# Two decoder layers with cached attention: scores from key tiles by TensorE column groups in place of VectorE products, one pair at a time

## The chip, the core and the metric

The kernel runs on one core of a Trainium2 chip. The metric is the device time of one execution in microseconds (us). The kernel before was run three times: 1359.86, 1361.52 and 1363.43 us, median 1361.52 us.

## What is computed

Two rows of activations (batch B = 2, one new token each, D = 448) go through the same two blocks twice: attention over a cache of 4096 keys and values in each of 16 heads (head size 256), and a gated feed-forward block (F = 1792). All is float32.

```
def _A_ref(x, k_cache, v_cache, wq, wo):          # attention, H = 16, Dh = 256
    q = (x @ wq).reshape(B, Sq, H, Dh).transpose(0, 2, 1, 3)
    scores = einsum("bhqd,bhkd->bhqk", q, k_cache) * (Dh ** -0.5)
    o = einsum("bhqk,bhkd->bhqd", softmax(scores), v_cache)
    return o.transpose(0, 2, 1, 3).reshape(B, Sq, H * Dh) @ wo
def _B_ref(x, W_gate, W_up, W_down):              # feed-forward
    gate, up = x @ W_gate, x @ W_up
    return ((gate * (gate > 0)) * up) @ W_down
x = x + _A_ref(layernorm(x), ...); x = x + _B_ref(layernorm(x), ...)
x = x + _A_ref(layernorm(x), ...); x = x + _B_ref(layernorm(x), ...)
```

The second layer uses the same caches and weights as the first, and all of them together are far larger than on-chip memory, so nearly everything is read from HBM twice.

## The kernel before

**Pairs and pieces.** The work of one layer's attention is 32 pairs (head, batch row). Keys and values of a pair are 4 MB each. Each is cut into four pieces of 128 partitions x 2048 floats (1 MB; 8 KB in each partition): partition p holds 32 consecutive keys, a piece is 8 of them, each of 256 numbers.

**Places.** A tile `arena` has 27 places of one piece: 6 blocks of 4 and 3 singles (`BLOCKS`, `SINGLES`). A load takes a place, or a whole free block when four pieces are loaded by one DMA (`grouped`); it is put on SyncE's queue (SP) by `pump`, which runs each time that a piece is given back (`release`). So the loads stand in one fixed list, `pending`, and each is issued when its turn has come and its places are free. The list is: head weights, keys of pair 0, keys of pair 1, values of pair 0, keys of pair 2, values of pair 1 and so on, then the eleven weight pieces of the feed-forward block (seven `in`, four `out`), and the same for layer two, whose pairs run in reverse order. The first 13 and the last 12 pieces of a layer's caches go singly where the rules `SMALL` and `ENDS` say so.

**Kept pieces.** Because layer two starts with the pairs on which layer one ended, some pieces stay in the arena and are not loaded again: `KEPT = 20` pieces of keys and values and one more piece of values, and the weights of one head. While they lie there, 5 of the 27 places are left for loads.

**Scores.** `score(u, c)` works on piece c of pair u. VectorE multiplies the piece by the query, which stands on all 128 partitions (L360, one instruction of 2048 numbers per partition), then VectorE sums five of the eight keys (L365) and ScalarE three (L362). For kept pieces, whose contents must survive, VectorE does eight fused multiply-and-sum instructions instead (L354). The query is brought to all partitions by a TensorE product with 33 columns, a ScalarE copy and two GpSimd broadcasts (`query`), or by TensorE with the row repeated 128 times (`query_of`).

**Softmax, values, output.** `softmax_max` and `softmax_exp` find the maximum (VectorE, GpSimd), the exponentials (ScalarE, L378 and L381) and their sum (GpSimd). `weigh` multiplies with the values on TensorE, four products of 2 x 512 per piece in four column groups of the array (L401: `po[32*t : 32*t+2]`). `out_copy`, `out_add`, `out_turn`, `out_keep`, `project` bring a pair's result through `wo` into `acc` (L414, L417, L425, L434, L444). `absorb` adds the result to the activations, `squares` and `deviation` do the layer norm, `ffn` the feed-forward block (L498 for gate and up, L525 and L527 turn the hidden row, L568 and L573 for down).

**Order.** The order is written by hand. Step u of the loop at L463 scores pair u, weighs pair u-1 and turns and projects pair u-2, interleaved, so a layer's end is two steps behind its last scores. `busy` issues TensorE products into `po_all` whose results nobody reads (L222): 8 squares of 128 x 128 after each piece of the last two weighed pairs of a layer, and a few before the feed-forward block.

Of the kernel before, what the change touches and what calls it, by code (L numbers as in the profile page):

```python
# [8 lines left out]
F32 = mybir.dt.float32  # L9
# [14 lines left out]
KEPT = 20  # L24
# [4 lines left out]
BY_ACT = 3  # L29
HEAD = FULL * DH + P + 2 * D  # L30
# [35 lines left out]
def two_layers(  # L66
# [19 lines left out]
    ps_f = ctx.enter_context(tc.tile_pool(name="ps_f", bufs=2, space=PSUM))  # L86
# [10 lines left out]
    def source(key, n):  # L97
        kind, name, c = key
        if kind in "kv":
            h, b = name  # L100
            rows = (k_cache if kind == "k" else v_cache)[b, h]
            return rows.rearrange("(p t) d -> p (t d)", t=NT)[:, c * UNIT : (c + n) * UNIT]
# [65 lines left out]
    keep.add(("v", second[2], NC - 1))  # L168
# [9 lines left out]
    junk = consts.tile([P, DH], F32, name="junk")  # L178
# [22 lines left out]
    xs = consts.tile([P, DC, 33], F32, name="xs")  # L201
    nc.vector.memset(xs, 0.0)
    xr = xs[:, :, :32].rearrange("p c (b r) -> p c b r", b=B)
# [7 lines left out]


# [3 lines left out]

    def busy(n, half):


        for k in range(0, n, 4):  # L220
            m = min(4, n - k)
            nc.tensor.matmul(  # L222
                po_all[:B, half, : m * P], ident[:, :B],
                ident[:, None, :].to_broadcast([P, m, P]), start=True, stop=True,
            )
# [10 lines left out]
    def absorb(rows, n, rhs, nrhs):  # L236


        sums = work.tile([P, 1], F32, name="sums")
        nc.scalar.activation(row[:n, :D], rows, AF.Copy, accum_out=sums[:n])  # L240
        minus = ps_s.tile([P, B], F32, name="small")
        nc.tensor.matmul(minus, sums[:n].to_broadcast([n, P]), nrhs[:n], start=True, stop=True)
        pt = ps_s.tile([P, DC, B], F32, name="small")
        turned(pt, row[:n], rhs[:n], start=True, stop=True)
        less = work.tile([P, B], F32, name="less")
        nc.vector.tensor_copy(less, minus)
        for part in (less[:, None, :].to_broadcast([P, DC, B]), pt):
# [3 lines left out]
        nc.vector.tensor_copy(xs[:, :, 32:], xs[:, :, 31:32])  # L251
# [20 lines left out]
    def attention(order, after, begun):  # L272
# [8 lines left out]
        def query_of(u, pq):  # L281
            h, b = order[u]
            w = get("h", h, 0)
            for c in range(FULL):
                nc.tensor.matmul(  # L285
                    pq[:, b, :],
                    xT[:, c, b : b + 1].to_broadcast([P, P]),
                    w[:, c * DH : (c + 1) * DH],
                    start=(c == 0),
                    stop=False,  # L290
                )
            for j in range(2):
                nc.tensor.matmul(
                    pq[:, b, j * P : (j + 1) * P],
                    xT[:, FULL + j, b : b + 1].to_broadcast([P, P]),
                    w[:, FULL * DH : FULL * DH + P],
                    start=False,
                    stop=(j == 1),
                )
            q_of[u] = pq[:, b, :]  # L300

        def query(u):
            h = order[u][0]
            w = get("h", h, 0)
            pq = ps_q.tile([P, B, DH], F32, name="pq")
            if ("h", h, 0) in after:
                for v in (u, u + 1):
                    query_of(v, pq)
                return


            q = pq[:33, 0, :]
            for c in range(FULL):
                nc.tensor.matmul(  # L314
                    q, xs[:, c, :], w[:, c * DH : (c + 1) * DH], start=(c == 0), stop=False
                )
            for j in range(2):
                nc.tensor.matmul(  # L318
                    q[:, j * P : (j + 1) * P],
                    xs[:, FULL + j, :],  # L320
                    w[:, FULL * DH : FULL * DH + P],
                    start=False,
                    stop=(j == 1),
                )
            found = w[:33, DH : 2 * DH]
            nc.scalar.activation(found, q, AF.Copy)  # L326
            for v in (u, u + 1):
                b = order[v][1]
                q_of[v] = w[:, 2 * b * DH : (2 * b + 1) * DH]
                nc.gpsimd.partition_broadcast(q_of[v], found[32 * b : 32 * b + 1], channels=P)  # L330

        def first_query():


            total = squares()
            pq = ps_q.tile([P, B, DH], F32, name="pq")
            w = get("h", order[0][0], 0)
            for u, at in ((0, HEAD), (1, 0)):
                query_of(u, pq)
                nc.scalar.activation(w[:, at : at + DH], q_of[u], AF.Copy)  # L340
                q_of[u] = w[:, at : at + DH]
                if u == 0:
                    deviation(total)
            nc.scalar.activation(nsr[:, :1], eps_t, AF.Exp)

        def score(u, c):
            kt = get("k", order[u], c).rearrange("p (t n) -> p t n", t=CT)
            if c == 0:
                s_of[u] = work.tile([P, NT], F32, name="scores")
            kept = ("k", order[u], c) in after  # L350
            found = s_of[u][:, c * CT : (c + 1) * CT]
            if kept or ahead and u < ahead:
                for t in range(CT):
                    nc.vector.scalar_tensor_tensor(  # L354
                        junk if kept else kt[:, t, :], kt[:, t, :], 1.0, q_of[u],
                        op0=ALU.mult, op1=ALU.mult, accum_out=found[:, t : t + 1],
                    )
            else:

                nc.vector.tensor_mul(kt, kt, q_of[u][:, None, :].to_broadcast([P, CT, DH]))  # L360
                for t in range(BY_ACT):
                    nc.scalar.activation(  # L362
                        kt[:, t, :], kt[:, t, :], AF.Copy, accum_out=found[:, t : t + 1]
                    )
                nc.vector.reduce_sum(found[:, BY_ACT:], kt[:, BY_ACT:, :], axis=AX.X)  # L365
            if not kept:
                release("k", order[u], c)
# [25 lines left out]
        def weigh(u, c):  # L393
# [16 lines left out]
            if u >= n_u - 2:  # L410
                busy(8, (u + 1) % 2)
# [24 lines left out]
        def project(u):  # L436
# [11 lines left out]
            if u == n_u - 1:  # L448
                busy(5, 0)
# [8 lines left out]
        begun()  # L458

        ahead = 2 if ("k", order[0], 0) in keep else 0  # L460
        if ahead:
            query(ahead)
        for u in range(n_u + 2):  # L463
            if_pair(score, u, 0)
            if u == 0:
                inverse()
                nc.vector.tensor_scalar_mul(sr, rstd, SCALE)
                nc.vector.tensor_scalar_mul(nsr, rstd, -SCALE)
            if_pair(out_add, u - 2)
            if_pair(out_turn, u - 2)  # L470
            if_pair(score, u, 1)
            if_pair(score, u, 2)
            if_pair(out_keep, u - 2)
            if_pair(project, u - 2)
            if u % 2 and ahead < u + 1 < n_u:
                query(u + 1)
            if_pair(softmax_sum, u - 1)
            if_pair(score, u, 3)
            if_pair(softmax_max, u)
            if_pair(softmax_exp, u)  # L480
            for c in range(NC):
                if_pair(weigh, u - 1, c)
            if_pair(out_copy, u - 1)

    def ffn(last):
# [3 lines left out]
        busy(2, 0)  # L489
        total = squares()  # L490

        def proj(parts):

            p = ps_f.tile([P, D], F32, name="pf")
            for n, (part, c, done) in enumerate(parts):
                w = get("in", "", part)
                for j in range(4):
                    nc.tensor.matmul(  # L498
                        p[32 * j : 32 * j + 32, :],
                        xs[:, c, :32],  # L500
# [10 lines left out]
        pg = proj([(0, 0, True), (1, 1, True), (2, 2, True), (3, 3, False)])  # L511
# [8 lines left out]
        pu = proj([(3, 4, True), (4, 0, True), (5, 1, True), (6, 2, True)])  # L520
        nc.vector.tensor_mul(hid, pu, hid)

        ph = ps_f.tile([P, 4, P], F32, name="pf")
# [19 lines left out]
        else:  # L543
# [3 lines left out]
            near = work.tile([P, FULL, 4, B], F32, name="near")  # L547
# [4 lines left out]
            near_tails = work.tile([P, 2, B], F32, name="near_tails")  # L552
# [6 lines left out]
        pd = ps_f.tile([P, D], F32, name="pf")  # L559
# [39 lines left out]
def _arrays(np, A_x, A_k_cache, A_v_cache, A_wq, A_wo, B_W_gate, B_W_up, B_W_down, **_):  # L599
# [11 lines left out]
    chunks += [np.concatenate([down[j, rows:], down[j + 1, rows:]]) for j in (0, 2)]  # L611
    found = {
        "x": A_x,
        "k_cache": A_k_cache,
# [30 lines left out]
```

## Time and profile before

| what | value |
|---|---|
| runs of the kernel before | 1359.86, 1361.52, 1363.43 us |
| the profiled execution: span from first to last instruction | 1357.3 us |
| VectorE busy (DVE) | 1012.7 us, 75% |
| TensorE busy (PE) | 583.2 us, 43% |
| ScalarE busy (ACT) | 407.8 us, 30% |
| mean clock granted to TensorE | 0.681 of full speed |
| bytes of the load queue | 562.58 MB |

The page of the profiled execution gives its span, not its time by the host's measure, so 2.6 to 6.1 us of the three times shown lie around the span. Of the trace, the most telling view here is the table of stretches: for chosen stretches it gives the busy time of each engine, the granted clock of TensorE (PEclk), the share of the time that the DMA engines were busy and the rate at which they moved bytes. A timeline row gives start, duration, engine, line, operation, what it writes and reads, and in brackets how long its engine had idled and what ended that. In the trace a float32 product is two MATMUL and two weight-load records.

### The profile page before, as it was taken

The page shows a single profiled execution, that of the slowest core. Times are in us where ns is not written, and L with a number is a line of the kernel's source. Part 1 is how long each engine was busy: PE and PEld are TensorE (multiplying, and loading weights), DVE is VectorE, ACT ScalarE, POOL GpSimd, SP SyncE. Part 2 cuts the span into 40 slices and gives each one's busy share as a digit, 9 for nine tenths or more (in the row PEclk, how much of TensorE's full clock was granted, in tenths as well). Part 3 has the DMA queues.
Part 4 walks back from the last instruction along what each step waited for, and adds up shares of the span by engine and source line. Part 5 has one row for each costly group of instructions (what it writes and reads, how often), then busy time and mean ns, then how long its engine had stood idle before and what let it go on. Part 6 is the DMA issues. An engine that isn't in the chain of part 4 may idle for free.

```text
span 1357.3 us, 10287 instructions
## 1 busy us (share of the span) xinstructions
PE 583.2 (43%) x3122; PEld 189.5 (14%) x3122; DVE 1012.7 (75%) x1183; ACT 407.8 (30%) x1733; POOL 106.8 (8%) x192
## 2 busy tenths in 40 slices
PE   2433424434334444245773444434434434334368
PEld 2111101111101111012130111111101111111112
DVE  4987787777877877877339999987877877877861
ACT  2333333333333333320011333333333333333321
POOL 0210000000000000000001111110000000000010
PEclk9767566667667666567796666666566667666679
DMA  9999999999999999999879999999999999999994
GB/s 400 434 431 430 432 430 432 430 429 431 431 430 432 430 430 429 431 428 424 344 307 361 402 431 432 433 429 429 431 427 434 429 430 433 429 428 436 422 421 167
DMA packets 29294, 563.22 MB, mean 415 GB/s; under 512 B 3252, under 2 KB 3384, under 8 KB 10168
## 3 DMA queue, kind: packets, MB, share of 16 engines
q1 hardware_dynamic: 29236, 562.58, 97.3%
q8 instruction: 24, 0.39, 0.1%
q14 instruction: 30, 0.25, 0.0%
q10 hardware_dynamic: 4, 0.00, 0.0%
HBM read 562.56 MB, written 0.00 MB: 414 GB/s over the span
## 4 chain that ended last, share of the span: by engine, by line
DMA 53%; DVE 32%; PE 11%; ACT 2%; issue 2%; DVEq 0%; POOL 0%; SPq 0%; POOLq 0%; ACTq 0%
DMA arena<-in_k_cache_dram 52%; DVE arena L360 16%; DVE scores L365 11%; PE pq L314 2%; PE po L222 2%; PE acc L444 2%; DVE junk L354 2%; DVE arena L354 1%; PE po L401 1%; ACT arena L362 1%; DVE row L417 1%; PE pf L498 1%; DMA arena<-in_w_out_dram 1%; PE pq L285 1%; PE pq L318 1%
## 5 line engine op out<-in xcount | busy, mean ns | idle before, releaser
L360 DVE TENSOR_TENSOR arena<-arena 128x2048 f32<-128x2048 f32 x236 | 539.4, 2285 | 152.1 <-DMA arena<-in_k_cache_dram 147.3
L362 ACT ACTIVATE arena<-arena 128x256 f32<-128x256 f32 x708 | 286.0, 405 | 538.5 <-DVE arena L360 538.5
L401 PE MATMUL po<-arena,probs 128*2 128x512 f32 x2048 | 315.1, 738 | 122.3 <-DMA arena<-in_v_cache_dram 112.6
L365 DVE TENSOR_REDUCE scores<-arena 128x5 f32<-128x1280 f32 x236 | 350.7, 1486 | 8.2
L425 PE MATMUL small<-ones,row 128*128 128x1 f32 x256 | 62.2, 347 | 416.3 <-DVE row L417 416.3
L444 PE MATMUL acc<-arena,oT 128*2 128x448 f32 x128 | 51.6, 905 | 195.0 <-DVE oT L434 195.0
L362 ACT ACTIVATION_READ_ACCUMULATOR arena<-arena 128x1 f32 x708 | 132.5, 187 | 0.0
L425 PEld LDWEIGHTS small<-ones,row 128*128 128x128 f32 x256 | 56.7, 309 | 477.1 <-DVE row L417 477.1
L401 PEld LDWEIGHTS po<-arena,probs 128*2 128x2 f32 x2048 | 54.6, 96 | 318.1 <-issue 307.6
L373 POOL PARTITION_ALL_REDUCE top<-mx x64 | 51.5, 805 | 595.0 <-DVE mx L371 595.0
L314 PE MATMUL pq<-arena,xs 128*33 128x256 f32 x174 | 75.1, 599 | 13.8 <-DMA arena<-in_w_head_dram 12.6
L330 POOL PARTITION_BROADCAST arena<-arena x58 | 30.0, 587 | 536.1 <-ACT arena L326 509.6
L371 DVE TENSOR_REDUCE mx<-scores 128x1 f32<-128x32 f32 x64 | 11.9, 186 | 69.6 <-ACT arena L362 66.1
L378 ACT ACTIVATE nm<-top,nsr 128x1 f32<-128x1 f32 x64 | 18.8, 294 | 146.4 <-POOL top L373 146.4
L417 DVE SCALAR_TENSOR_TENSOR row<-po,ri,row 128x256 f32<-128x256 f32 x64 | 30.5, 477 | 39.5 <-ACT row L414 39.4
L326 ACT ACTIVATE arena<-pq 33x256 f32<-33x256 f32 x29 | 10.9, 377 | 140.6 <-PE pq L318 140.6
L414 ACT ACTIVATE row<-po,ri 128x256 f32<-128x256 f32 x64 | 29.6, 462 | 52.1 <-PE po L222 38.0
L314 PEld LDWEIGHTS pq<-arena,xs 128*33 128x33 f32 x174 | 25.5, 163 | 82.9 <-issue 80.1
L222 PE MATMUL po<-ident 128*2 128x512 f32 (+2 forms) x76 | 36.9, 609 | 0.0
L354 DVE SCALAR_TENSOR_TENSOR junk<-arena,pq 128x256 f32<-128x256 f32 x64 | 26.9, 420 | 8.0 <-DMA arena<-in_k_cache_dram 6.0
L444 PEld LDWEIGHTS acc<-arena,oT 128*2 128x2 f32 x128 | 3.0, 82 | 197.7 <-DVE oT L434 197.7
L385 POOL PARTITION_ALL_REDUCE total<-rs x64 | 24.6, 385 | 61.7 <-ACT probs L381 61.7
(105 smaller groups left out, 284.0 us busy)
## 6 DMA issues: line engine op xcount, KB each, us to landing
arena<-in_k_cache_dram SPq DMA_DIRECT2D x57, 4096.0 KB, 44.7
arena<-in_v_cache_dram SPq DMA_DIRECT2D x57, 4096.0 KB, 53.0
arena<-in_w_head_dram SPq DMA_DIRECT2D x31, 896.0 KB, 39.4
arena<-in_v_cache_dram SPq DMA_DIRECT2D x19, 1024.0 KB, 19.9
arena<-in_k_cache_dram SPq DMA_DIRECT2D x16, 1024.0 KB, 9.1
arena<-in_w_in_dram SPq DMA_DIRECT2D x14, 896.0 KB, 18.6
arena<-in_w_out_dram SPq DMA_DIRECT2D x4, 896.0 KB, 13.0
arena<-in_w_out_dram SPq DMA_DIRECT2D x3, 672.0 KB, 7.8
```

Source lines behind the costliest of these rows:

```text
L222: nc.tensor.matmul(po_all[:B, half, : m * P], ident[:, :B], ident[:, None, :].to_broadcast([P, m, P]), start=True, stop=True,)
L314: nc.tensor.matmul(q, xs[:, c, :], w[:, c * DH : (c + 1) * DH], start=(c == 0), stop=False)
L330: nc.gpsimd.partition_broadcast(q_of[v], found[32 * b : 32 * b + 1], channels=P)
L354: nc.vector.scalar_tensor_tensor(junk if kept else kt[:, t, :], kt[:, t, :], 1.0, q_of[u], op0=ALU.mult, op1=ALU.mult, accum_out=found[:, ...
L360: nc.vector.tensor_mul(kt, kt, q_of[u][:, None, :].to_broadcast([P, CT, DH]))
L362: nc.scalar.activation(kt[:, t, :], kt[:, t, :], AF.Copy, accum_out=found[:, t : t + 1])
L365: nc.vector.reduce_sum(found[:, BY_ACT:], kt[:, BY_ACT:, :], axis=AX.X)
L373: nc.gpsimd.partition_all_reduce(mx_of[u], mx, P, RED.max)
L401: nc.tensor.matmul(po_of[u][32 * t : 32 * t + 2, :], p_of[u][:, n : n + 2], vt[:, 2 * t * DH : (2 * t + 2) * DH], start=(c == 0), stop=(c ...
L417: nc.vector.scalar_tensor_tensor(row[:, :DH], po_of.pop(u)[:, DH:], r_of[u][:, 1:2], row[:, :DH], op0=ALU.mult, op1=ALU.add,)
L425: nc.tensor.matmul(pT_of[u][:, c : c + 1], row[:, c * P : (c + 1) * P], ones, start=True, stop=True,)
L444: nc.tensor.matmul(acc[at : at + B], oT_of[h][:, c, :], wo[:, c * D : (c + 1) * D], start=(n < 3), stop=(n >= n_u - 3),)
```

## The change

Keys are laid out on the host so that a piece holds, on partition p, number p (and number 128 + p) of each of 1024 keys. The query is made as a column: `query` multiplies the head's weights (as the stationary operand) with the activations and copies a 128 x 4 result from PSUM. `score` is then 8 TensorE products per piece: the query column is stationary (one column), 256 keys move, two halves of the head are added up, and four groups of keys go to four column groups of the array, rows 0, 32, 64 and 96 of the PSUM tile `raw`. The piece is given back as soon as these are done. VectorE copies 128 x 256 of `raw` (of which four rows matter) to `found_s`, and `score_turn` turns that with two TensorE products of 128 x 4 per piece into the layout that the softmax had before. The multiplication and sums on VectorE and ScalarE are gone, as are the GpSimd broadcasts.

The loop does a pair from scores to weighing in one step: scores, softmax, then output steps of the pair before, the next query, then weighing, and in the list of loads the values of a pair follow its keys. `busy` and its products are gone. `KEPT` is 22 (the extra piece of values is dropped), so 22 pieces and one head stay and 4 places are left. The feed-forward block uses `raw` in place of two PSUM tiles of its own.

```diff
-KEPT = 20
+KEPT = 22
+G, E = 4, 2
+QN = E * P
...
         for u, unit in enumerate(order):
             found.append(("k", unit, 0))
-            if u > 0:
-                found.append(("v", order[u - 1], 0))
             if u % 2 and u + 1 < len(order):
                 found.append(("h", order[u + 1][0], 0))
-        return found + [("v", order[-1], 0)]
+            found.append(("v", unit, 0))
+        return found
...
-    keep.add(("v", second[2], NC - 1))
...
+            pq = ps_q.tile([P, 2, B], F32, name="pq")
+            for j in range(2):
+                for c in range(FULL):
+                    at = c * DH + j * P
+                    nc.tensor.matmul(
+                        pq[:, j, :], w[:, at : at + P], xT[:, c, :], start=(c == 0), stop=False
+                    )
...
+            nc.vector.tensor_copy(q, pq)
...
         def score(u, c):
...
+            kt = get("k", order[u], c).rearrange("p (j g n) -> p j g n", j=2, g=G)
+            half, at = c % 2, c // 2 * QN
+            for j in range(2):
+                for g in range(G):
+                    nc.tensor.matmul(
+                        raw[32 * g : 32 * g + 1, half, at : at + QN],
+                        q_of[u][:, j, :], kt[:, j, g, :], start=(j == 0), stop=(j == 1),
+                    )
+            if ("k", order[u], c) not in after:
+                release("k", order[u], c)
+            nc.vector.tensor_copy(found_s[:, half, :], raw[:, half, at : at + QN])
+
+        def score_turn(u, c):
...
+            for e in range(E):
+                n = c * CT + e * G
+                nc.tensor.matmul(
+                    s_of[u][:, n : n + G], found_s[:, c % 2, e * P : (e + 1) * P], pick,
+                    start=True, stop=True,
+                )
...
-            if u >= n_u - 2:
-                busy(8, (u + 1) % 2)
...
-            if u == n_u - 1:
-                busy(5, 0)
...
+        for u in range(n_u + 1):
             if_pair(score, u, 0)
...
+            for c in range(1, NC):
+                if_pair(score, u, c)
+                if_pair(score_turn, u, c - 1)
+            if_pair(score_turn, u, NC - 1)
             if_pair(softmax_max, u)
             if_pair(softmax_exp, u)
+            if_pair(out_turn, u - 1)
+            if_pair(out_keep, u - 1)
+            if_pair(project, u - 1)
+            if u % 2 and u + 1 < n_u:
+                query(u + 1)
             for c in range(NC):
...
+                if_pair(weigh, u, c)
+            if_pair(softmax_sum, u)
+            if_pair(out_copy, u)
+            if_pair(out_add, u)
```

On TensorE, in the middle of a layer, two pairs before: `po` is the weighing, `small` the turning of a result row, `acc` the projection, `pq` the query.

```order
L401 MATMUL po<-arena,probs 2x512 x16
L425 MATMUL small<-ones,row 128x1 x2
L444 MATMUL acc<-arena,oT 2x448 x2
L314 MATMUL pq<-arena,xs 33x256 x3
L318 MATMUL pq<-arena,xs 33x128 x2
L401 MATMUL po<-arena,probs 2x512 x16
L425 MATMUL small<-ones,row 128x1 x2
```

One pair and its output steps now; `raw` are the scores (L308), `small<-ident,found_s` their turning (L321).

```order
L308 MATMUL raw<-arena,q 1x256 x16
L321 MATMUL small<-ident,found_s 128x4 x2
L308 MATMUL raw<-arena,q 1x256 x8
L321 MATMUL small<-ident,found_s 128x4 x2
L308 MATMUL raw<-arena,q 1x256 x8
L321 MATMUL small<-ident,found_s 128x4 x4
L380 MATMUL small<-ones,row 128x1 x2
L399 MATMUL acc<-arena,oT 2x448 x2
L358 MATMUL po<-arena,probs 2x512 x16
```

A pair's 16 weighing products now stand behind 40 products of its own scores. On the same engine at the end of layer two, before, the last weighed pieces alternate with the unread products (L222).

```order
L401 MATMUL po<-arena,probs 2x512 x4
L222 MATMUL po<-ident 2x512 x2
L425 MATMUL small<-ones,row 128x1 x2
L444 MATMUL acc<-arena,oT 2x448 x2
L222 MATMUL po<-ident 2x512
L222 MATMUL po<-ident 2x128
L242 MATMUL small<-nlead,sums 128x2
```

Now the same place reads so.

```order
L358 MATMUL po<-arena,probs 2x512 x16
L380 MATMUL small<-ones,row 128x1 x2
L399 MATMUL acc<-arena,oT 2x448 x2
L238 MATMUL small<-nlead,sums 128x2
L226 MATMUL small<-lead,row 128x2 x3
L228 MATMUL small<-lead,row 64x2 x2
L447 MATMUL raw<-arena,xs 32x448 x16
```

Between the last weighing and the feed-forward block (L447, before L498) only the output steps are left. On SyncE's queue around the change of layers, before:

```order
L123 DMA arena<-in_v_cache_dram 128x8192
L123 DMA arena<-in_k_cache_dram 128x2048 x4
L123 DMA arena<-in_v_cache_dram 128x2048 x8
L123 DMA arena<-in_w_in_dram 128x1792 x7
L123 DMA arena<-in_w_out_dram 128x1792
```

and now:

```order
L127 DMA arena<-in_k_cache_dram 128x8192
L127 DMA arena<-in_v_cache_dram 128x2048 x4
L127 DMA arena<-in_k_cache_dram 128x2048 x4
L127 DMA arena<-in_v_cache_dram 128x2048 x4
L127 DMA arena<-in_w_in_dram 128x1792 x7
L127 DMA arena<-in_w_out_dram 128x1792
```

The values of the last pair but one moved ahead of the last pair's keys; the feed-forward weights still follow the last values.

More of the change, by code (lines that the diff above doesn't have):

```diff
@@ L278, in attention @@
         n_u = len(order)
[L281 to L300, printed above, removed]
         def query(u):
@@ L348, in score @@
-            if c == 0:
[L349 to L365, printed above, removed]
@@ L546, in ffn @@
             nc.vector.tensor_mul(square, rstd, rstd)
-            near = work.tile([P, FULL, 4, B], F32, name="near")
+            near = row[:, D : D + 12 * B].rearrange("p (m j b) -> p m j b", m=FULL, j=4)
             nc.vector.tensor_mul(
@@ L551, in ffn @@
             )
-            near_tails = work.tile([P, 2, B], F32, name="near_tails")
+            near_tails = row[:, D + 12 * B : D + 14 * B].rearrange("p (m b) -> p m b", m=2)
             nc.vector.tensor_mul(
```

107 lines of the change are left out of this document (31 added, 76 removed).

## The prediction

> **What bounds the kernel now.** I read the page first, then the stretches, then single rows. The page shows what is full:
>
> ```profile
> span 1357.3 us, 10287 instructions
> PE 583.2 (43%) x3122; PEld 189.5 (14%) x3122; DVE 1012.7 (75%) x1183; ACT 407.8 (30%) x1733; POOL 106.8 (8%) x192
> ...
> q1 hardware_dynamic: 29236, 562.58, 97.3%
> q8 instruction: 24, 0.39, 0.1%
> ```
>
> VectorE is the busiest engine, but the load queue's packets fill 97.3% of the time of the 16 DMA engines. Where they are not full is told by the stretches (columns: window, length, PE, PEld, DVE, ACT, POOL busy, PEclk, DMA share, GB/s):
>
> ```profile
> 0.00:40.00 40.00, 12.07 (x42) 8.37 (x43) 20.62 (x33) 10.87 (x33) 1.77 (x7) 0.88 0.97 408
> 40.00:600.00 560.00, 222.31 (x1184) 69.49 (x1186) 438.29 (x360) 181.93 (x791) 42.79 (x84) 0.64 1.00 430
> 600.00:640.00 40.00, 16.99 (x96) 7.54 (x92) 28.59 (x130) 3.74 (x14) 1.47 (x4) 0.67 1.00 424
> 640.00:677.00 37.00, 25.67 (x125) 6.22 (x118) 17.49 (x84) 2.43 (x8) 1.47 (x4) 0.80 0.89 369
> 677.00:688.00 11.00, 9.67 (x64) 3.68 (x62) 2.29 (x12) 2.39 (x4) 0.00 (x0) 1.00 0.18 55
> 688.00:702.00 14.00, 9.38 (x70) 2.52 (x69) 1.74 (x6) 1.14 (x4) 0.00 (x0) 0.88 0.99 385
> 702.00:716.00 14.00, 8.15 (x49) 5.82 (x46) 9.84 (x56) 3.42 (x8) 1.33 (x2) 1.00 0.96 388
> 716.00:737.00 21.00, 7.20 (x40) 2.01 (x44) 20.76 (x94) 3.16 (x13) 3.52 (x4) 0.59 1.01 384
> 737.00:760.00 23.00, 6.71 (x38) 1.75 (x32) 22.62 (x21) 8.89 (x40) 2.62 (x2) 0.65 0.83 347
> 760.00:1300.00 540.00, 220.53 (x1204) 70.01 (x1200) 435.60 (x359) 180.46 (x787) 51.11 (x84) 0.66 1.00 430
> 1300.00:1317.40 17.40, 12.35 (x51) 2.63 (x52) 9.13 (x9) 4.44 (x21) 0.73 (x2) 0.70 1.01 421
> 1317.40:1340.30 22.90, 20.48 (x120) 6.51 (x122) 3.23 (x16) 3.09 (x7) 0.00 (x0) 1.00 0.87 356
> 1340.30:1357.30 17.00, 11.68 (x69) 2.97 (x61) 2.49 (x9) 1.80 (x6) 0.00 (x0) 1.00 0.00 0
> ```
>
> Two stretches of 550 us run at 430 GB/s with a DMA share of 1.00: DMA is the bound, and a faster engine gains nothing in them. 562.58 MB at 430 GB/s are 1308.3 us. A stretch loses its length times (1 - rate/430): 2.6 us in the first 40 and in 600 to 640, **24.3 us from 640 to 760** (5.2, 9.6, 1.5, 1.4, 2.2, 4.4: the change of layers), and 21.3 after 1300. Together 1356.5, the span within 1 us. So the change can win only by fewer bytes, at the change of layers, and at the end.
>
> **What is removed in the long stretches is worth nothing there, if TensorE can carry it.** A pair needs 8.39 MB and half a head (0.46 MB): 20.6 us at 430 GB/s. TensorE's rows, at half and at full clock:
>
> ```profile
> 415.42 3.86 PE L401 MATMUL po<-arena,probs 128*2 128x512 f32 x32
> 429.94 5.13 PE L401 MATMUL po<-arena,probs 128*2 128x512 f32 x32 [4.46 <-DMA arena<-in_v_cache_dram]
> 402.78 1.01 PE L425 MATMUL small<-ones,row 128*128 128x1 f32 x4 [8.70 <-DVE row L417]
> 1319.23 0.61 PE L425 MATMUL small<-ones,row 128*128 128x1 f32 x4 [1.08 <-DVE row L417]
> 410.28 1.66 PE L444 MATMUL acc<-arena,oT 128*2 128x448 f32 x4 [6.49 <-DVE oT L434]
> 1332.17 0.92 PE L444 MATMUL acc<-arena,oT 128*2 128x448 f32 x4 [0.25 <-DVE oT L434]
> ```
>
> Weighing takes 3.9 us at full clock (5.13 begins at half; twice 3.9 bounds it). Scoring moves as many columns, 32 products of 256 against 16 of 512: 3.9 us if four column groups run abreast as there. No row shows products this short abreast, so: at least 3.9, at most 13.7 (64 records one after another at half of the 0.43 us that a lone 512-column record takes), taken 3.9 to 6.9, the rate of the weighing's 0.107 us a record; the end is the same for both. Eight score turns, like four times L425: 2.4 us full, 4.0 half. Result turn 0.6 or 1.0. Projection and query (eight products, also four L425) fall to every second pair: 1.7 or 2.8. The softmax chain and the last VectorE copy, during which TensorE has the result turn, projection or query: 0.5 left over. **12.9 us full** (15.9 with the dear scoring), 24.5 half at most. At the full clock there are 5 to 8 us to spare, at the half it is 4 short, but a TensorE that never idles does not stay there:
>
> ```profile
> 405.74:409.16 3.42, 0.00 (x0) 0.00 (x0) 3.38 (x3) 1.01 (x7) 0.00 (x0) 0.50 1.03 438
> 412.57:415.98 3.41, 3.41 (x13) 1.34 (x15) 1.66 (x2) 0.45 (x2) 0.00 (x0) 0.50 1.01 432
> 415.98:419.39 3.41, 3.31 (x32) 0.57 (x24) 0.19 (x1) 1.95 (x10) 1.69 (x4) 1.00 1.03 442
> 419.39:422.81 3.42, 0.00 (x0) 0.00 (x0) 2.56 (x2) 0.71 (x2) 0.00 (x0) 1.00 0.98 422
> 422.81:426.22 3.41, 1.01 (x4) 0.93 (x4) 3.41 (x3) 1.04 (x6) 0.00 (x0) 0.50 0.98 416
> ```
>
> After one window of 3.41 us in which it was busy throughout, the clock was 1.00; after an idle one 0.50. So 1080 us of VectorE and ScalarE score work cost nothing today but at the change of layers, and go unrewarded elsewhere; the cover is the load queue. The added waits are hidden by it too: on VectorE the first copy of a pair stands behind `out_add`, which waits for `out_copy` behind the last weighing (0.5 us each, 1.7 us with the latencies), while TensorE does two pieces of scores (1.9); on TensorE the next pair's scores stand behind the wait for the exponentials.
>
> **Bytes.** 22 pieces stay instead of 21: 1.05 MB, **-2.4 us**. More TensorE instructions must be fetched: some 18,000 for 10,287, of whose 0.39 MB above that makes 0.3 MB more, +0.7 us.
>
> **The change of layers.** These rows tell it; the last values of layer one land at 646.5 + 19.8 = 666.3:
>
> ```profile
> L123 SPq DMA_DIRECT2D arena<-in_v_cache_dram x1: 328/328/328, 646.5 to 646.5; - x1
> DMA to landing us min/median/max: 19.8/19.8/19.8
> 678.63 0.47 ACT L414 ACTIVATE row<-po,ri 128x256 f32<-128x256 f32 x1 [11.61 <-PE po L222]
> 684.12 3.21 PE L498 MATMUL pf<-arena,xs 128*32 128x448 f32 x32
> 685.13 1.68 SPq L123 DMA_DIRECT2D arena<-in_w_in_dram  x2
> L354 DVE SCALAR_TENSOR_TENSOR junk<-arena,pq 128x256 f32<-128x256 f32 x64 | 26.9, 420 | 8.0 <-DMA arena<-in_k_cache_dram 6.0
> ```
>
> All free places are full by 677; the first comes back when L498 begins, 17.8 us after 666.3, for two pairs are weighed then with unread products between (the 11.61 us wait on L222). Changed: the last piece is weighed 0.9 to 1.7 us after it lands, 5.5 us lead from L414 to L498 at full clock, 8.5 with the TensorE part of it (3 us) at half, and one weight piece takes 0.8 to 1.5: a place comes back after 7.2 to 11.7 us. Four pieces in four places keep DMA for 8.5. A restart costs some 2.6 us (this queue's load at 685.1 landed 4.7 later, of which 2.1 is transfer). Loss 1.3 to 5.8; I take 6, since with single pieces coming every 2.45 us TensorE will be at half clock; with 0.9 for the lower rate of single pieces 6.9 where 14.8 stood (640 to 688). From 688 to 716 2.9 us were lost; one place fewer is 2.4 more, while a score piece comes back after 0.9 to 1.7 us instead of 4.0 (eight L354 of 0.42 and a read each): 2.9 to 5.3, taken 5.3. From 716 to 760 VectorE was the bound (22.62 busy of 23.00); eight pieces take TensorE 13 to 16 us where DMA needs 19.5, so of 6.6 lost there 0.9 to 6.6, taken 1.9, stay. Sum 14.1 for 24.3: **-10.2** (-5.5 to -18).
>
> **The end.** Before, the last values land at 1297.5 + 19.8 = 1317.3 and the span ends 40.0 later.
>
> ```profile
> L123 SPq DMA_DIRECT2D arena<-in_v_cache_dram x1: 328/328/328, 1297.5 to 1297.5; - x1
> L222 PE MATMUL po<-ident 128*2 128x512 f32 (+2 forms) x76 | 36.9, 609 | 0.0
> 1335.76 3.21 PE L498 MATMUL pf<-arena,xs 128*32 128x448 f32 x32
> 1355.02 0.33 SPq L593 DMA_DIRECT2D out_dram<-row  x1
> ```
>
> Half of the 36.9 us of unread products lie between. Changed: L498's successor begins 6.4 to 10.2 us after the landing, and from L498 to the end it was 21.5 us (1335.8 to 1357.3) at full clock; the weights arrive in time but for 2 us in the fastest case. 30 to 35.4 (one window of 3.4 at half clock inside costs half of it), taken 34: **-6.0** (-4.6 to -10).
>
> **Sum.** 1357.3 - 2.4 + 0.7 - 10.2 - 6.0 = 1339.4 of span; with 4.2 us around it (1361.5 - 1357.3; the runs shown lie 2.6 to 6.1 above) **1343.6**, own range 1330 to 1352.
>
> **Rivals.**
> *Full clock throughout* (0.10): scores and weighing run together and the clock never falls at the two ends. Terms at their better ends: 1330 to 1336. Against it: the 0.00 windows above, one after almost every burst.
> *The layers change as slowly as before* (0.13): four places instead of five, and what a faster score gives back waits for the feed-forward block anyway. The 10.2 stay: 1353.8. For it: 55 GB/s from 677 to 688 comes from that block's start, not from scores. Against: the wait on L222 goes.
> *TensorE becomes the bound* (0.10, **slower**): column groups with one stationary column run one after another. Scoring 13.7, a pair 22.7 at full clock, 2.1 over 20.6 in each of 64 pairs: about +135 us, 1480. It decides from 11.6 us of scoring a pair. Against: L401 runs four groups abreast in the same kind of tile. The Trainium skill ("TensorE: Matmul & The Clock Gate", "Wait — 56ns, not 53.3ns?") has a rule against this change: without hardware decode the sequencer needs about 62 ns a MATMUL, which binds when the array needs less. By that estimate, charged to weight loads as well, scoring is 7.9 us and the sum stays; no run here shows it.
> *Half clock through both feed-forward blocks* (0.05, slower): without unread products TensorE never fills a window there, and its 16.2 us from L498 to the end (11.68 in the last stretch, 4.5 before it) double. The end grows to 49 us (+9) and the change of layers keeps its 24.3: 1369. It decides where waits for weights break up L498. The rows at 412.57 and 415.98 speak against it, since L498 alone is busy for 3.2 us at a stretch. The same page of the Trainium skill ("HAM oscillation — how this bites in real kernels") says that a kernel which waits for DMA longer than a window at every tile runs each of them cold; that would be this case, and this trace has the half clock after an idle window too.
>
> **How the numbers follow.** Forecast 0.58, the four rivals 0.38, better than 1330 the last 0.04. Likeliest 1344. The range 1331 to 1358 leaves out the slow rivals and the best end. A measurement can tell about 0.3% from no change, 4.1 us: faster below 1357.4 gets 0.82, slower above 1365.6 0.13, same 0.05.
>
> **What would show it.** Right: 430 GB/s in the long stretches, TensorE waiting for keys in most pairs, scores near 1 us a piece at full clock, no stretch at 55 GB/s longer than 6 us at the change of layers, the feed-forward block of layer two 6 to 10 us after the last values. Wrong: loads waiting for score products in mid-layer (then the third rival), or PEclk 0.50 through L498's successor (the fourth).

## The result and the profile after

| kernel | median us (lowest to highest) | ratio to before, 95% interval |
|---|---|---|
| before | 1361.33 (1359.86 to 1363.43) | 1 |
| changed | 1347.03 (1346.09 to 1348.22) | 0.9902 [0.9886, 0.9918] |

The forecast was 1344 us, range 1331 to 1358. The profiled execution of the changed kernel took 1346.37 us. Its page (span; busy time of engines; granted clock and rate in 40 slices; load queue and instruction queue; the chain that ended last; two groups):

```profile
span 1344.6 us, 18672 instructions
PE 1077.4 (80%) x8328; PEld 476.1 (35%) x8328; DVE 203.3 (15%) x676; ACT 93.4 (7%) x284; POOL 47.7 (4%) x134
...
PEclk9867776667767776766778896876776777677678
...
GB/s 398 432 431 431 428 428 432 431 427 428 430 433 432 429 429 427 431 432 421 403 255 400 436 428 431 431 427 431 429 429 434 428 429 429 429 434 429 426 418 252
...
q1 hardware_dynamic: 29524, 561.53, 98.0%
q8 instruction: 65, 1.06, 0.3%
...
PE 65%; DMA 15%; another core or an unknown queue 14%; DVE 3%; issue 2%; ACT 1%; SPq 0%; POOL 0%; POOLq 0%; DVEq 0%; ACTq 0%
...
L308 PE MATMUL raw<-arena,q 128*1 128x256 f32 x4096 | 360.2, 481 | 176.3 <-DMA arena<-in_k_cache_dram 140.0
L358 PE MATMUL po<-arena,probs 128*2 128x512 f32 x2048 | 343.9, 812 | 48.0 <-DMA arena<-in_v_cache_dram 43.1
```

VectorE has gone from 75% to 15% busy and TensorE from 43% to 80%, for about 1% of the time. Two readings of this page disagree. The chain puts 65% on TensorE; the queue is full at 98.0%, and TensorE's score products (L308) waited 140.0 us for keys. The experiments with doubled work below decide between them. The stretches, cut as in the prediction (same columns) but for the last, which ends at 1290:

```profile
40.00:600.00 560.00, 457.41 (x3484) 202.38 (x3476) 81.09 (x260) 33.84 (x109) 19.81 (x54) 0.71 1.00 430
640.00:677.00 37.00, 32.10 (x234) 14.55 (x238) 6.80 (x27) 4.38 (x11) 1.47 (x4) 0.70 0.88 364
677.00:688.00 11.00, 7.07 (x56) 1.84 (x52) 0.49 (x3) 0.70 (x2) 0.00 (x0) 0.93 0.88 320
688.00:702.00 14.00, 10.87 (x71) 6.02 (x63) 2.82 (x12) 1.07 (x4) 0.00 (x0) 0.77 0.81 323
702.00:716.00 14.00, 11.83 (x101) 4.88 (x105) 2.95 (x11) 2.51 (x6) 0.73 (x2) 0.74 0.66 257
716.00:737.00 21.00, 19.79 (x191) 8.87 (x183) 3.90 (x13) 1.71 (x5) 0.73 (x2) 0.84 1.01 421
737.00:760.00 23.00, 22.10 (x203) 11.40 (x206) 4.74 (x17) 2.00 (x7) 1.47 (x4) 0.86 1.03 437
760.00:1290.00 530.00, 419.92 (x3374) 184.06 (x3366) 78.83 (x252) 32.60 (x105) 19.08 (x52) 0.74 1.00 429
```

The long stretches did not move: 430 and 429 GB/s. The time came from the two ends. By the prediction's measure, length times (1 - rate/430), the change of layers (640 to 760) loses 17.7 us where it lost 24.3: 8.5 from 640 to 688 (14.8 before), **9.1 from 688 to 716 (2.9 before)**, 0.1 from 716 to 760 (6.6 before). The 55 GB/s hole is gone, and a new one, 257 GB/s, stands later. At the end of layer two, the group of the last value load (its issue, and the time to its landing) reads:

```profile
L127 SPq DMA_DIRECT2D arena<-in_v_cache_dram x1: 327/327/327, 1292.0 to 1292.0; - x1
...
DMA to landing us min/median/max: 19.8/19.8/19.8
```

So the last values land at 1311.8 and the span ends 32.8 us later, where it was 40.0. Bytes -2.4, instruction fetch +1.6 (0.67 MB more on q8), change of layers -6.6 and end -7.2 make -14.6. The span is 12.7 shorter; of the 1.9 us between, 1.2 are the 530 us that ran at 429 instead of 430 GB/s.

### The profile page after: what moved, and what is told of

Its sections match the earlier page's. It is cut to its first block, busy times and chain, and to the rows that moved or that the text cites. A ratio compares the mean times of both kernels' runs of the same rounds, so it can differ in the third digit from the quotient of the medians.

```text
span 1344.6 us, 18672 instructions
## 1 busy us (share of the span) xinstructions
PE 1077.4 (80%) x8328; PEld 476.1 (35%) x8328; DVE 203.3 (15%) x676; ACT 93.4 (7%) x284; POOL 47.7 (4%) x134
## 3 DMA queue, kind: packets, MB, share of 16 engines
q1 hardware_dynamic: 29524, 561.53, 98.0%
## 4 chain that ended last, share of the span: by engine, by line
PE 65%; DMA 15%; another core or an unknown queue 14%; DVE 3%; issue 2%; ACT 1%; SPq 0%; POOL 0%; POOLq 0%; DVEq 0%; ACTq 0%
PE raw L308 22%; PE po L358 20%; PE small L321 11%; DMA arena<-in_k_cache_dram 11%; PE pq L283 4%; DMA arena<-in_w_head_dram 4%; PE small L380 2%; PE acc L399 2%; DVE found_s L314 2%; PE pq L286 1%; PE raw L447 1%; DMA arena<-in_w_in_dram 1%; PE raw L517 0%; PE acc L522 0%
## 5 line engine op out<-in xcount | busy, mean ns | idle before, releaser
L308 PE MATMUL raw<-arena,q 128*1 128x256 f32 x4096 | 360.2, 481 | 176.3 <-DMA arena<-in_k_cache_dram 140.0
L358 PE MATMUL po<-arena,probs 128*2 128x512 f32 x2048 | 343.9, 812 | 48.0 <-DMA arena<-in_v_cache_dram 43.1
L308 PEld LDWEIGHTS raw<-arena,q 128*1 128x1 f32 x4096 | 91.9, 91 | 376.3 <-issue 147.1
L321 PEld LDWEIGHTS small<-ident,found_s 128*128 128x128 f32 x1024 | 176.2, 248 | 123.1 <-issue 118.8
L321 PE MATMUL small<-ident,found_s 128*128 128x4 f32 x1024 | 196.2, 301 | 0.3
L314 DVE COPY found_s<-raw 128x256 f32<-128x256 f32 x256 | 108.6, 424 | 475.1 <-PE raw L308 474.6
L283 PE MATMUL pq<-xs,arena 128*128 128x2 f32 x384 | 71.6, 303 | 0.4 <-DVE xs L246 0.4
L283 PEld LDWEIGHTS pq<-xs,arena 128*128 128x128 f32 x384 | 68.9, 263 | 1.9 <-DVE total L256 1.5
L330 POOL PARTITION_ALL_REDUCE top<-mx x64 | 22.5, 351 | 1184.7 <-DVE mx L328 1152.3
L286 PE MATMUL pq<-xs,arena 128*128 128x2 f32 x128 | 30.4, 307 | 0.0
L286 PEld LDWEIGHTS pq<-xs,arena 128*128 128x128 f32 x128 | 28.0, 270 | 0.0
L342 POOL PARTITION_ALL_REDUCE total<-rs x64 | 24.5, 383 | 63.5 <-ACT probs L338 63.5
L338 ACT ACTIVATE probs<-small,nm,sr 128x32 f32<-128x32 f32 x64 | 24.1, 377 | 2.1
L447 PE MATMUL raw<-arena,xs 128*32 128x448 f32 x128 | 16.6, 661 | 5.4 <-DMA arena<-in_w_in_dram 3.1
```

Source lines behind the costliest of these rows:

```text
L283: nc.tensor.matmul(pq[:, j, :], w[:, at : at + P], xT[:, c, :], start=(c == 0), stop=False)
L286: nc.tensor.matmul(pq[:, j, :], w[:, FULL * DH : FULL * DH + P], xT[:, FULL + j, :], start=False, stop=True,)
L308: nc.tensor.matmul(raw[32 * g : 32 * g + 1, half, at : at + QN], q_of[u][:, j, :], kt[:, j, g, :], start=(j == 0), stop=(j == 1),)
L314: nc.vector.tensor_copy(found_s[:, half, :], raw[:, half, at : at + QN])
L321: nc.tensor.matmul(s_of[u][:, n : n + G], found_s[:, c % 2, e * P : (e + 1) * P], pick, start=True, stop=True,)
L342: nc.gpsimd.partition_all_reduce(r_of[u], rs, P, RED.add)
```

## The experiments

All ratios are to the kernel before, run on the same chip in the same set of runs.

### Is it the scores, or the unread products?

The unread products were taken out of the kernel before, and nothing else:

```diff
-            if u >= n_u - 2:
-                busy(8, (u + 1) % 2)
...
-            if u == n_u - 1:
-                busy(5, 0)
...
-        busy(2, 0)
```

> The kernel before, with its unread products left out and nothing else changed. Ends theory: the unread products behind the last two weighed pairs are what delayed both feed-forward blocks; the block of layer two begins 7 to 10 us after the last values in place of 18.5, that of layer one likewise, and VectorE still binds behind the change of layers: 1344 to 1350 us, that is nearly the whole gain of the change (1347.0) without one score product on TensorE. Rival (scores theory: VectorE's scores of the last pairs hold up the end of the layer, the unread products only fill time that is waited anyway): 1357 to 1362.

Measured: 1345.22 us, ratio 0.9879 [0.9863, 0.9896]. And they were put back into the changed kernel (the same lines with a plus, and the function `busy`):

> The changed kernel with the unread products put back at the same places (eight squares after each piece of the last two pairs' weighing, seven before the feed-forward block). Ends theory, with one pair in hand at a time: only the last pair's weighing lies behind the last values, so they cost 4 pieces x 1.7 us less what the full clock gives back (2.5 us) at each end: 1349 to 1355 us. If the whole gain of the change were their removal: 1359 to 1362. If they only kept the clock up: 1342 to 1345.

Measured: 1362.46 us, ratio 1.0012 [1.0001, 1.0022]. The stretch of the change of layers that differs most, with SyncE's first load in the feed-forward block (the first place given back); first the old scores without unread products:

```profile
677.00:688.00 11.00, 8.47 (x63) 2.56 (x55) 1.11 (x4) 0.70 (x2) 0.00 (x0) 0.81 0.92 337
```

then the new scores with them, and their span:

```profile
span 1356.8 us, 18824 instructions
...
677.00:688.00 11.00, 9.24 (x74) 3.93 (x78) 2.70 (x14) 2.76 (x6) 0.00 (x0) 1.00 0.34 123
...
683.14 1.83 SPq L127 DMA_DIRECT2D arena<-in_w_in_dram  x3
```

and the changed kernel:

```profile
676.83 2.78 SPq L127 DMA_DIRECT2D arena<-in_w_in_dram  x3
```

The old scores without unread products already run at 337 GB/s where the hole of 55 was. With them, PEclk is 1.00 from 677 to 688 and the first place comes back 6.3 us later; the end after the last landing is 38.2 us instead of 32.8. They bought a faster clock (the block's first 32 records took 3.21 us in place of 4.91), which does not repay them. So removing them alone gives the whole gain of the change, and adding them to the change takes all of it away. My expectation for the second run (part of the gain, 1349 to 1355) was too mild.

### What 22 kept pieces cost

First 21 pieces kept instead of 22, then, with 22 kept, the two heads one entry sooner in the list of loads:

```diff
-KEPT = 22
+KEPT = 21
```

> The changed kernel with 21 pieces kept in place of 22, nothing else. Places theory: the loss of 9.1 us from 688 to 716 comes from the list of loads, in which a key piece that finds no block place stands ahead of two head loads that would find a free single place; with 21 kept there are three block places for the three pieces ahead of the heads, so the heads load at once. It costs 1.05 MB (+2.4 us) and gives back 4 to 6 us: 1343 to 1346 us, 1 to 4 under the changed kernel's 1347.0, and in the trace no stretch near 0 GB/s between the feed-forward weights and the first returned key place. Rival (the loss there is the TensorE path at half clock, places do not matter): 1349 to 1350, by the bytes alone.

```diff
-    of_second[NC - 1 : NC - 1] = heads
+    of_second[NC - 2 : NC - 2] = heads
```

> The changed kernel with the two head loads of layer two put behind two cache pieces in the list in place of three; 22 pieces kept, the same bytes. Places theory: the two heads (1.83 MB, 4.3 us of DMA) load into the free single places while the third cache piece waits for a block place; of the 3.5 us at 9 GB/s most goes: 1343 to 1345 us. Rival (half clock on the path to the first scores sets it, the heads only change their place in the list): 1346.5 to 1347.5.

Measured: 1340.76 us, ratio 0.9854 [0.9838, 0.9871] with 21 kept, although it loads 1.05 MB more: better than my own theory had it, and faster than both kernels. The heads sooner: 1344.62 us, ratio 0.9888 [0.9870, 0.9906], which overlaps the changed kernel's interval, so the time settles nothing. The traces say more. The changed kernel has two holes here, and SyncE's loads (start, duration, operation, how many) stand beside them:

```profile
695.20:698.00 2.80, 2.01 (x18) 1.10 (x14) 0.37 (x3) 0.63 (x2) 0.00 (x0) 0.93 0.50 132
703.50:707.00 3.50, 2.98 (x26) 0.71 (x22) 0.59 (x2) 0.94 (x2) 0.00 (x0) 0.67 0.08 9
...
695.59 1.16 SPq L127 DMA_DIRECT2D arena<-in_v_cache_dram  x2
705.96 0.33 SPq L127 DMA_DIRECT2D arena<-in_k_cache_dram  x1
706.34 0.90 SPq L127 DMA_DIRECT2D arena<-in_w_head_dram  x2
```

with the heads sooner:

```profile
697.91 1.60 SPq L127 DMA_DIRECT2D arena<-in_v_cache_dram  x2
699.56 0.91 SPq L127 DMA_DIRECT2D arena<-in_w_head_dram  x2
708.31 3.61 SPq L127 DMA_DIRECT2D arena<-in_k_cache_dram  x3
```

and with 21 kept, with its stretches:

```profile
686.84 4.89 SPq L127 DMA_DIRECT2D arena<-in_v_cache_dram  x3
692.84 1.96 SPq L127 DMA_DIRECT2D arena<-in_w_head_dram  x2
702.33 5.10 SPq L127 DMA_DIRECT2D arena<-in_k_cache_dram  x4
...
640.00:677.00 37.00, 31.95 (x244) 13.99 (x240) 7.07 (x27) 4.39 (x11) 1.47 (x4) 0.73 0.94 389
677.00:688.00 11.00, 7.83 (x63) 2.24 (x55) 1.11 (x4) 0.70 (x2) 0.00 (x0) 0.93 0.89 327
688.00:702.00 14.00, 10.55 (x82) 5.13 (x80) 2.87 (x15) 2.82 (x7) 0.00 (x0) 0.89 1.01 423
702.00:716.00 14.00, 11.49 (x113) 4.23 (x112) 2.90 (x9) 1.24 (x4) 0.74 (x2) 0.86 0.98 371
```

With 22 kept, the first cache pieces of layer two in the list are two of values and one of keys; the keys find no place until the first scores of layer two give one back at 705.96, and both heads stand behind them: that is the second hole, some 5.5 us. The first, some 3.3 us from 692 to 698, stands before it, while the values themselves wait for a place until 695.59. With the heads sooner they go out at 699.56 and the second hole is gone (373 to 416 GB/s from 702 to 708), but the first one is longer, since the values find a place only at 697.91 in that trace, which is of the second longest of its six runs (1348.33) and has the granted clock at 0.50 from 690 to 698. With 21 kept three pieces of values go out at 686.84 and the heads follow, and neither hole is there: the loss from 688 to 716 is 2.1 us instead of 9.1, and from 640 to 688 it is 6.2 instead of 8.5.

Then 20 kept, and 21 kept together with the heads sooner:

> The changed kernel with 20 pieces kept, four block places free behind the change of layers. Places theory: 21 kept already lets the loads run on (371 to 438 GB/s from 702 us); one more place gains at most what is left of 702 to 716 us (2 us), and the piece loaded once more costs 1.05 MB / 430 = 2.4 us: 1339 to 1344 us, about as 21 kept (1340.8). Rival (more places, always less loss, as 22 to 21 gave 6.3 us): 1334 to 1337 us. Against both: above 1345 us would say that 21 kept was luck of the list's order and not places.

> 21 pieces kept and the two heads one entry sooner in the list of loads. Theory of places: with three block places free nothing stands behind an entry that waits for a place between 688 and 702 us (423 GB/s there with 21 kept), so the heads' order changes nothing: 1339 to 1343 us, as 21 kept alone (1340.8). Rival (the heads' order is worth the 2.4 us that it gave with 22 kept): 1337 to 1339 us.

Measured: 1341.78 us, ratio 0.9858 [0.9844, 0.9873] with 20, and 1343.69 us, ratio 0.9875 [0.9859, 0.9891] for the pair of edits, 0.7 us above what I expected. So with a third block place the order of the heads gains nothing, and one place is enough: in its trace the next one wins 1.5 us of rate from 640 to 760, less than its 2.4 us of bytes.

### How much cover TensorE still has

The turn products of every piece were issued twice, then three times, and in another kernel the score products twice. Nothing else is touched in any of the three:

```diff
-            for e in range(E):
+            for e in (0, 1, 0, 1):
```

> The changed kernel with the turn products of every piece issued a second time (1024 records more, 3.07 us a pair by the 196.2 us of the changed kernel's 1024). Cover theory: TensorE is idle about 4.2 us of the 20.6 us of a pair (80% busy in 1344.6 us), so the work lies beside the loads: the long stretches stay at 430 GB/s, only the pairs next to the two ends pay, 1347 to 1353 us, TensorE about 93% busy. Rival (TensorE sets the pace already, as 65% of the chain that ended last would read): all 64 pairs pay, 1347 + 196 = about 1543 us; half that if half the pairs do.

```diff
-            for e in range(E):
+            for e in (0, 1, 0, 1, 0, 1):
```

> The same with the turn products three times: 6.1 us a pair more against about 4.2 us of room. Cover theory: at the clock of the changed kernel (0.74) TensorE becomes the bound, 64 x 1.9 = some 120 us more, 1467 us, with the long stretches near 395 GB/s; if the clock is granted more often as TensorE stays busy (one turn of a piece 0.61 us at full clock, so 64 x 4 x 2 x 0.61 = 312 us more of work than 1077 less what full clock saves) it still fits, below 1360 us. Which of the two comes tells what the clock does under a TensorE that never pauses.

```diff
-            for j in range(2):
+            for j in (0, 1, 0, 1):
```

> The changed kernel with the score products of every piece issued a second time: 32 records of 256 columns a piece instead of 16, 1.04 us a piece more at full clock, 4.2 us a pair, against 4.9 us a pair at full clock (8 x 0.61) for the run with the turn products three times, which took 1454.7 us at a granted clock of 0.73 with TensorE 94% busy. Theory of moved columns (the clock is granted by how many columns stream through the array in a window, and turns, 4 columns behind a 128-column weight load, count as rest): the clock rises above the 0.74 of the changed kernel, to 0.85 or more, a pair takes 13.0 + 4.2 = 17 us of TensorE, inside 20.6, and the time is 1347 to 1360 us. Rival (the clock goes by how busy TensorE is, or has a fixed share): it stays at 0.72 to 0.76, a pair takes 16.7 + 5.5 = 22 us, and the time is 1430 to 1460 us.

Measured: 1354.27 us (ratio 0.9957 [0.9937, 0.9977]) with turns twice, 1 us above the cover theory's range; 1454.74 us in the one run with turns three times; 1357.18 us (0.9967 [0.9955, 0.9979]) with scores twice. Turns twice:

```profile
PE 1182.6 (88%) x9352; PEld 628.6 (47%) x9352; DVE 201.3 (15%) x676; ACT 93.6 (7%) x284; POOL 47.9 (4%) x134
...
40.00:600.00 560.00, 494.60 (x3889) 264.85 (x3881) 80.20 (x260) 33.89 (x109) 19.90 (x54) 0.73 1.00 430
```

The page gives 105 us more TensorE work, and the rate of the long stretch stays at 430: DMA bounds the changed kernel there, and the chain's 65% for TensorE names work that lies along the path there but does not set its length. The cover is thin, though, as the third copy shows. Turns three times, and then scores twice:

```profile
PE 1368.3 (94%) x10376; PEld 835.2 (57%) x10376; DVE 198.6 (14%) x676; ACT 93.5 (6%) x284; POOL 47.9 (3%) x134
...
PEclk9777776767766776777776767766776767766778
```

```profile
PE 1149.9 (85%) x12424; PEld 502.1 (37%) x12424; DVE 204.2 (15%) x676; ACT 93.4 (7%) x284; POOL 47.7 (4%) x134
...
PEclk9889888798888898888878999898897888888898
```

At one clock the two additions are nearly the same: 4.9 us a pair for two more turns, 4.2 for the scores again, at full clock. One costs 108 us and the other 10, because the mean granted clock is 0.727 in the first and 0.882 in the second. Busy time times mean clock is nearly one amount of work, 995 and 1014 us; at the clock of the first the second would be busy for some 1395 us and no longer fit beside the loads.

### What grants the clock

The rows of the kernel with turns three times, cut at the 3.41 us grid on which its clock changes, and TensorE's timeline there:

```profile
307.39:310.80 3.41, 3.41 (x47) 2.18 (x39) 0.61 (x2) 0.00 (x0) 0.00 (x0) 1.00 0.98 423
310.80:314.22 3.42, 3.42 (x39) 2.74 (x39) 0.67 (x2) 0.00 (x0) 0.00 (x0) 1.00 0.96 407
314.22:317.63 3.41, 3.41 (x18) 3.41 (x18) 0.19 (x1) 0.00 (x0) 0.25 (x1) 0.50 1.08 461
317.63:321.05 3.42, 3.42 (x17) 3.42 (x17) 0.16 (x1) 0.76 (x3) 0.48 (x2) 0.50 0.96 414
321.05:324.46 3.41, 3.41 (x17) 0.65 (x21) 0.46 (x3) 0.00 (x0) 0.00 (x0) 0.50 0.91 385
324.46:327.87 3.41, 2.82 (x39) 0.68 (x35) 0.82 (x2) 0.47 (x1) 0.00 (x0) 1.00 1.12 477
```

```profile
309.50 1.04 PE L308 MATMUL raw<-arena,q 128*1 128x256 f32 x16
310.48 1.50 PE L321 MATMUL small<-ident,found_s 128*128 128x4 f32 x12
311.91 1.04 PE L308 MATMUL raw<-arena,q 128*1 128x256 f32 x16
312.88 4.09 PE L321 MATMUL small<-ident,found_s 128*128 128x4 f32 x24
...
317.69 1.42 PE L283 MATMUL pq<-xs,arena 128*128 128x2 f32 x6
...
321.17 5.22 PE L358 MATMUL po<-arena,probs 128*2 128x512 f32 x32
```

TensorE's matrix work is without a pause from 307 to 324, and the clock still falls to 0.50 at 314.22, behind a window with one piece of scores and some 2.4 us of turns. It stays at 0.50 through two windows of turns and query products, in which the weight loads (PEld) are busy for the whole window and 4, 2 or 1 columns move behind each, and comes back at 324.46, behind the window of weighing, whose products move 512 columns. So a busy TensorE is not enough: in these kernels the clock follows how many columns move. The count bears it out. In 79 windows of this grid from 303.98 us on, the columns of scores, weighing and projection were added up, with four column groups abreast taken as one: all 41 windows with 1536 or fewer were followed by 0.50, and 34 of the 38 with 1792 or more by 1.00. In the changed kernel, over 89 windows from 303 us on, it is 46 of 46 and 38 of 43; there 18 windows in which TensorE was busy throughout were followed by half clock, and 23 in which it was busy for less than 3.05 us by full clock. The Trainium skill ("TensorE: Matmul & The Clock Gate", "What's actually happening") has the gate set by how busy TensorE has recently been, and its window of 3413 ns agrees with the grid here; "busy" as the page of the profile counts it is not what is watched, since 94% busy had the lower clock and 85% the higher. No experiment set the number of columns on purpose, so the limit is known only to lie above 1536 by this rough count.

One attempt used this at the ends: 21 kept, and one unread product of 512 columns after each of the first three value pieces of a layer's last pair:

```diff
-KEPT = 22
+KEPT = 21
...
+            if u == n_u - 1 and c < NC - 1:
+                busy(4, (u + 1) % 2)
```

> 21 pieces kept, and after each of the first three value pieces of a layer's last pair one unread product of 512 columns, so that TensorE pauses less just before the ends. Clock theory: the feed-forward block's first records then run at full clock (4.9 to about 3.2 us twice) and the four 0.9 us products hide in waits for values: up to 2.5 us less an end, 1336 to 1340 us. Rival (what is put before the ends is paid, as the run with all unread products put back showed, 15 us): 1341 to 1346 us.

Measured: 1346.36 us, ratio 0.9888 [0.9867, 0.9910], no better than 21 kept without them (0.9854). The trace shown is of its longest run (1351.37, of 1342.13 to 1351.37), and that of 21 kept alone is of its shortest (1338.89), so the rows differ by more than the medians. Its feed-forward block's first 32 records, in the row below, began 4.2 us later than with 21 kept alone (675.03) and took 5.28 us, so they still met half clock:

```profile
679.24 5.28 PE L459 MATMUL raw<-arena,xs 128*32 128x448 f32 x32 [0.36 <-DVE xs L256]
```

## Why the prediction was right, and which steps were not

- **The bound.** Right. The long stretches kept 430 and 429 GB/s, and the score work that left VectorE and ScalarE (1420.5 us busy together before, 296.7 now) went unrewarded there.
- **TensorE can carry it.** Right in the result, wrong in the margin. A piece of scores, 16 records, takes 1.04 us at full clock, so the column groups run abreast and the rival with TensorE as the bound (about 1480) falls. But TensorE was busy 457.41 of 560 us, 82%, or 16.8 us of each 20.6, not the 12.9 that stood for full clock, since the granted clock was 0.71. (The six terms of that sum add up to 13.0, and the half-clock ones to 23.9 in place of 24.5; neither touches the forecast.) The sentence that a TensorE that never idles does not stay at half clock is refuted by turns three times.
- **The sequencer's 62 ns (the Trainium skill, "TensorE: Matmul & The Clock Gate", "Wait — 56ns, not 53.3ns?").** The estimate of 7.9 us of scoring a pair, charged to weight loads as well, does not hold here: four pieces of 1.04 us are 4.2 us at full clock. At half clock a piece took 1.89 us, so the price is mostly the array's and not a fixed one per record.
- **Bytes and fetch.** Bytes -2.4 right (562.58 to 561.53 MB); fetch +0.7 was +1.6, since q8 grew by 0.67 MB and not 0.3.
- **Change of layers, -10.2: mis-sized, -6.6.** 640 to 688 lost 8.5 for 6.9 forecast, 716 to 760 lost 0.1 for 1.9. The term that was off is **688 to 716: 9.1 for 5.3**. I priced the kept piece as one place fewer, 2.4 us, and did not ask which load would have to wait for a place and what is queued behind it. The values waited first (some 3.3 us of hole), then the keys, with both heads behind them, until layer two's first scores (some 5.5 us). The runs with 21 kept put the whole price of the 22nd piece at 6.3 us net of the bytes that it saves.
- **The end, -6.0:** -7.2, inside its range. The feed-forward block began 8.4 us after the last values, within the 6.4 to 10.2, and its first records partly met half clock (4.90 us, not 3.21):

```profile
1320.20 4.90 PE L447 MATMUL raw<-arena,xs 128*32 128x448 f32 x32 [0.36 <-DVE xs L246]
...
1326.94 3.21 PE L447 MATMUL raw<-arena,xs 128*32 128x448 f32 x32 [0.78 <-ACT row L468]
```

  From there to the end it was 24.4 us, not the 21.5 that the estimate kept. Half clock is 1.7 of the difference. The rest is a term that the prediction did not have: before the change the up projection followed the gate without a wait, and now it waits 0.78 us for ScalarE to have read the gate out of `raw`, with some 0.5 us more at the next such step. That this comes from the one tile `raw` in place of two is likely and was not tested. (The prediction's upper bound of 35.4 is not what its terms give, 10.2 + 21.5 + 1.7 = 33.4; the 32.8 measured lies under both.)
- **The sum.** The span came out 5.2 us above the forecast 1339.4, and the time around it was 1.8 us in the profiled execution, not 4.2; so 2.4 us of the miss cancelled by luck, and 1343.6 looks nearer than its steps were. The 4.2 set the span of one execution against the times of others; taken run by run, 1.7 to 3.1 us lie around the span, mostly 1.8.
- **Other rivals.** *Full clock throughout* falls with 0.71 and 0.74; *half clock through both feed-forward blocks* with PEclk 0.93 from 677 to 688 and with the 3.21 us at 1326.94; *the layers change as slowly as before* with the missing hole.
- **What the change is worth by its parts.** Unread products out: 16.1 us (1361.3 to 1345.2). The prediction counted this inside the change of layers and the end and never priced it alone. New scores, one pair at a time and the new list, with 21 pieces as before: 4.5 us more (to 1340.8); the two intervals overlap, so this part is not clear of the noise, and the three were not taken apart. In the traces it stands from 716 to 760, where VectorE had been the bound: the old scores without unread products lose 5.4 us there, the new ones with 21 kept nothing. The 22nd piece: 6.3 us back (to 1347.0).

## What to carry to other kernels

When loads go out in one fixed list, price a place not by its bytes alone but by which load will find none, how long it waits and what stands behind it. Before filling an engine's pauses with unread work to keep its clock up, time the kernel without it: here it stood on the path at both ends and cost about as much as the whole change won. And when DMA is the bound, show an engine's spare time by doubling its work, not by its share of a chain.

## What was not expected of the hardware

Two kernels with almost the same added TensorE time at full clock, 4.9 and 4.2 us a pair, ran at 1454.7 and 1357.2 us. The one that was busier (94% against 85%) was granted the lower clock (0.727 against 0.882), and the windows above go with the columns moved: its additions were weight loads of 128 columns with 4 columns moving behind each, the other's were products of 256 moving columns.
